# Written order on every engine, and earlier value tiles and opening steps, in a four-layer attention kernel

## The chip, the cores and the metric

The kernel runs on one core of a Trainium2 chip. The metric is the device time of one execution in microseconds (us); less is better. A program of instructions is built ahead of time: TensorE (PE) does matmuls and transposes into PSUM, VectorE (DVE), ScalarE (ACT) and GpSimd (POOL) do everything elementwise, and SyncE (SP) issues most of the DMA transfers. Each engine takes its own instructions in the order in which the program holds them and waits, at each, for what it needs from the others.

## The reference

Four layers in a row, each with a residual: linear attention (A), infini attention (B), A and B again, on x of 2048 tokens x 512 features, 32 heads of 16.

```python
def _A_ref(x, wqkv, w_phi, wo):                       # x is layer-normalized
    q, k, v = heads(x @ wqkv)                         # 32 heads, Dh = 16
    pq, pk = q @ w_phi, k @ w_phi                     # per head
    phi = lambda t: concat([softmax(t), softmax(-t)]) # 32 features a head
    kv, z = phi(pk)^T @ v, sum over tokens of phi(pk)
    return (phi(pq) @ kv / (phi(pq) @ z + 1e-6)) @ wo

def _B_ref(x, wq, wk, wv, wo, beta):                  # N = 4 segments of L = 512 tokens
    g = sigmoid(beta); M = z = 0; phi = lambda t: where(t > 0, t + 1, exp(t))
    for s in range(N):
        p = softmax(qs @ ks^T * Dh**-0.5 + causal_mask)
        a_mem = phi(qs) @ M / (phi(qs) @ z + 1e-6)
        o[s] = g * a_mem + (1 - g) * (p @ vs)
        M, z = M + phi(ks)^T @ vs, z + sum of phi(ks)
    return o @ wo

for layer in (A, B, A, B): x = x + layer(layernorm(x))
```

Inputs and outputs are fp32.

## The kernel before

Every dense product is kept near fp32 by splitting both factors into a high and a low part (fp32r) and adding three products (`mm3`): a 128 x 512 tile of a projection is 12 matmuls of 512 columns. A token tile is 128 tokens; a chunk or segment is four of them. Splitting is always an ACT copy (high) and a DVE or POOL subtraction (low). Work is written as Python generators, which other generators advance by `next`: the code that advances them decides the order in which instructions are emitted.

**Linear attention** is class `LayerA`. `pass1` goes over four chunks in the order `SEGS`. In each it projects k and q tiles (`kproj`, `qproj`), turns k tiles into features, and adds the products of features and values to `kva` (`kv(0)` after the first two k tiles, `kv(1)` after the other two). A feature tile goes through ACT's copy out of PSUM, DVE's maxima and minima (`extremes`), two POOL subtractions (`differences`), ACT's `exp`, DVE's sums, a reciprocal, and a product shared between DVE and POOL (`scale_k`). q tiles are stored to DRAM (`pqs`) with their maxima. Meanwhile a side generator normalizes the next chunk (`norm_T`: rows by DMA, moments on DVE, `refine`, `normal` on ACT, transposed into columns by PE) and makes its value tiles (`v_tile`). `first` writes out the start of the very first chunk by hand. `pass2` goes over 16 tiles of q: transposes of the features, the product with `kva`, a division (`weigh`), transposes of the result (`turn`), the output projection, and the residual.

**Infini attention** is class `LayerB`. `opening` loads the first weights of q and k (`wqk`) and all of v (`bwv`), starts the first norm and fills constant rows (`start`). `steps` walks k from `BEGIN` = -31 over R = 5 steps for each of 32 half chunks (8 heads x 512 tokens go in two halves). In each step TensorE does a fifth of the logits (`attend`, "lg") and a fifth of the products whose row maxima are taken on DVE (`maxima`, "mx"). Between them stand the tasks of a table: `BEFORE` (k < 0), `FIRST` (segment 0), `GAPS` (1 and 2), `LAST` or `FINAL` (3). A cell such as `0.4 m0` means half chunk 0, step 4, memory update 0; `v3` is a value tile, `n` and `ln` a step of the next norm, `fin` a `finish`, `max` the maxima. The tail of `steps` (after the loop) does the last `finish`, the rest of `early`, `end_turn` and `end`, together with the beginning of the next linear layer's pass1 (`after`).

`prepare` runs beside the first pass1: it splits the five weight matrices that come later into high and low parts and stores them to DRAM. `load_w` of such kept weights reads them again, `wtiles` "w8" or "e8" receiving two DMAs of 1 MB. At the end of each linear layer the main program walks pass2 for `A20` steps and advances `opening` at every third step from k = 30 on; the rest of pass2 goes into `steps` before k = 2, as far as the budget `LEFT` (in ns of TensorE work) tells.

**What sets the order.** The program is built by a framework that may reorder instructions by a timeline of its own. The class `Ordered` wraps the engines and ties each instruction behind the one before it, but only while a flag says so:

```python
j = (ends if ordered[0] or back[0] else floor).get(self.engine)
```

`strict` does the same for TensorE. The flags are on in `first`, in the last chunk of each pass1, in pass2 and in the loop of `steps`; in the first three chunks of pass1, in most of `prepare` and in the tail of `steps` the framework orders ACT, DVE, POOL and SP (and TensorE in part).

Of the kernel before, what the change touches and what calls it, by code (L numbers as in the profile page):

```python
# [15 lines left out]
D = 512  # L16
# [21 lines left out]
LEFT = 44000  # L38
BEGIN = -31
MAXIMA = -9  # L40
A20 = 76
PREP = 6
EVERY = (2, 2)
# [7 lines left out]
0.1 max k2/2       | 0.3 k2~           | 0.4 m0  # L51
1.1 max q3/2       | 1.3 fin q3~       | 1.4 t1 k3/1
# [47 lines left out]
BEFORE = {-30: "ln0", -29: "ln0", -28: "ln0", -27: "ln0", -25: "q0", -23: "v0", -21: "k0", -20: "load", -19: "v1",  # L100
          -18: "n", -17: "v2 n", -16: "n", -15: "n n", -14: "q1 n", -13: "n", -12: "v3 n", -11: "n", -10: "k1 n",
# [4 lines left out]
def interleave_kernel(ctx, tc, x_in, a_wqkv, a_wphi, a_wo, b_wq, b_wk, b_wv, b_wo, b_beta,  # L106
# [25 lines left out]
    strict = [False]  # L132
    last = [None]
    ordered = [False]
    back = [False]
    ends = {}
    floor = {}
    put_off = [None]

# [13 lines left out]
    class Ordered:  # L153


# [3 lines left out]
        def __getattr__(self, op):  # L159
            f = getattr(self.engine, op)  # L160

            def call(*a, **k):
                i = f(*a, **k)  # L163
                j = (ends if ordered[0] or back[0] else floor).get(self.engine)
                if j is not None:
                    behind(i, j)
                ends[self.engine] = i
                return i
            return call
# [3 lines left out]
    def held(i):  # L173

        if strict[0] and last[0] is not None:
            behind(i, last[0])
        last[0] = i
        return i
# [24 lines left out]
    def constants():  # L203

        sync.dma_start(out=mask, in_=c_mask)
        sync.dma_start(out=eb, in_=b_beta.unsqueeze(0).broadcast_to([P, H]))
        act.activation(eb, eb, AF.Exp, scale=-1.0)
        dve.tensor_scalar(eb, eb, 1.0, None, op0=ADD)
        dve.reciprocal(gates[:, 1, :], eb)
        dve.tensor_scalar(gates[:, 0, :], gates[:, 1, :], -1.0, 1.0, op0=MUL, op1=ADD)  # L210
        for j in range(4):
            dve.tensor_copy(share[32 * j : 32 * j + 32, :], gates[32 * j : 32 * j + 32, 0, j:H:4])
        dve.tensor_scalar(share, share, -1.0, bd[:, 24:25], op0=ADD, op1=MUL)
        dve.tensor_scalar(share, share, 1.0, None, op0=ADD)
        dve.tensor_copy(ones, bd[0:32, 25:26].broadcast_to([32, P]))
# [19 lines left out]
    def bring(w, key, src=None, tag="w8", low=dve):  # L235
        hi, lo = wtiles(tag)
        w[:] = [hi, lo]
        if key in kept:
            for t, k in zip((hi, lo), kept[key]):
                dma(t, k)  # L240
                yield
            return
# [56 lines left out]
    def prepare():  # L299


        for _ in range(PREP):
            yield
        back[0] = True
        constants()
        back[0] = False
        for m, src in enumerate((b_wq, b_wk)):
            for kc in range(NC):
                raw = T2("xr", 3)
                sync.dma_start(out=raw, in_=src[kc * P : (kc + 1) * P, :])  # L310
                hi = T2("oh", OO, F32R)
                lo = T2("ol", OO, F32R)
                for e in range(2):
                    for r in range(2):
                        rv = raw.rearrange("p (c f r e d) -> p e r c d f", c=NC, f=2, r=2, e=2)[:, e, r]
                        hv = hi.rearrange("p (c f e d r) -> p e r c d f", c=NC, e=2, f=2, r=2)[:, e, r]
                        lv = lo.rearrange("p (c f e d r) -> p e r c d f", c=NC, e=2, f=2, r=2)[:, e, r]
                        back[0] = True
                        act.copy(hv, rv)
                        back[0] = False  # L320
                        pool.tensor_tensor(out=lv, in0=rv, in1=hv.bitcast(F32), op=SUB)
                        for _ in range(EVERY[m]):
                            yield
                for a, t in enumerate((hi, lo)):
                    dma(wqk[m][:, :, a, kc, :], t.rearrange("p (c x) -> p c x", c=NC))
        for key, src in (("awo", a_wo), ("bwv", b_wv), ("bwo", b_wo)):
            keep = [dtile((P, NC, D), nm(key)) for _ in range(2)]
            for kc in range(NC):
                raw = T2("xr", 3)
                sync.dma_start(out=raw, in_=src[kc * P : (kc + 1) * P, :])  # L330
                hi = T2("oh", OO, F32R)
                lo = T2("ol", OO, F32R)
                back[0] = True
                act.copy(hi, raw)
                back[0] = False
                pool.tensor_tensor(out=lo, in0=raw, in1=hi.bitcast(F32), op=SUB)
                for k, t in zip(keep, (hi, lo)):
                    dma(k[:, kc, :], t)
                for _ in range(EVERY[1]):
                    yield  # L340
            kept[key] = keep
# [134 lines left out]
    def v_tile(hT, w, vv, tag):  # L476
# [4 lines left out]
        for t in range(4):  # L481
            po = PS(*tag)
            yield from tok_proj(po, hT, t, w)
            act.copy(v[:, t, 0 : H * VW].rearrange("p (h e) -> p h e", e=VW)[:, :, 0:DH],
                           po.rearrange("p (h e) -> p h e", e=DH))
            yield
# [80 lines left out]
    class LayerA:  # L567
# [4 lines left out]
        def first(self, hT, vv, nxt):  # L572

            ordered[0] = strict[0] = True
# [39 lines left out]
            side = norm_T(self.xsrc, SEGS[1], nxt, "e8", slow=True, off=True)  # L614
            next(side)
# [7 lines left out]
            for t in range(4):  # L623
# [5 lines left out]
                for _ in range(NEXT[t]):  # L629
                    next(side)  # L630
# [4 lines left out]
            ordered[0] = strict[0] = False  # L635
            floor.update(ends)
            return wq, wk, wv, side

        def pass1(self, first):
            hTs, vv, nxt = [], [], []  # L640
            if first:
                wq, wk, wv, ahead = self.first(hTs, vv, nxt)
# [15 lines left out]
            kva = sp.tile([P, 8, 4 * VW], F32, tag="acc", bufs=1, name=nm("kva"))  # L658
            for n, s in enumerate(SEGS):
# [3 lines left out]
                def kproj(t, e=None):  # L663
# [5 lines left out]
                    mm = extremes(pk, T2("mm", 2, shape=(P, 2, H)))  # L669
                    if e is None:  # L670
                        f = differences(pk, mm)
                        exp(f)
                        es.append(scale_k(f))
                    else:
                        e[t] = differences(pk, mm)

                def qproj(t):
# [36 lines left out]
                def go(steps):  # L714
                    for step in steps.split():
                        yield from {"k": kproj, "q": qproj, "v": kv}[step[0]](int(step[1]))

                if n < NSEG - 1:
                    hTs, vv = [], []
                    spare = ("e8" if first else "w8") if n % 2 == 0 else None  # L720
                    side = norm_T(self.xsrc, SEGS[n + 1], hTs, spare)
                    if first and n == 0:
                        hTs, side = nxt, ahead
                    side = chain(side, v_tile(hTs, wv, vv, ("g", G)))
                    steps = "k0 q0 k1 q1 v0 k2 q2 k3 q3 v1"
                    strict[0] = first and n == 0
                    if strict[0]:
                        steps = "k0 k1 q0 q1 v0 k2 k3 q2 q3 v1"
                    if n == 0 and not first:
                        yield from go("k0 k1 v0 k2 k3 v1")  # L730
                        wq = load_w("awq", None, "e8")
                        steps = "q0 q1 q2 q3"
                    if n == NSEG - 2:
                        steps, late = steps[:-3], kv(1)
                    for i, _ in enumerate(go(steps)):
                        next(side, None)
# [3 lines left out]
                    for _ in side:  # L740
                        yield
                    continue

                e = {}
                ordered[0] = strict[0] = True

                for t in range(8):
                    yield from (kproj(t, e) if t < 4 else qproj(t - 4))
# [76 lines left out]
    class LayerB:  # L825
# [6 lines left out]
        def start(self):  # L832
            self.mem = sp.tile([P, NC, 2, 8 * VW], F32, tag="acc", bufs=1, name=nm("mem"))
            self.sets = []
            for b in range(NSET):
                Q, K = [T2("e8", 2 * NSET, F32R, (P, 4, 512)) for _ in range(2)]
                self.sets.append((Q, K))
                for t, rows in ((Q, mask[0:32, 0:P]), (K, ones)):
                    dma(t[3:P:4].rearrange("p a t -> p (a t)"), rows.unsqueeze(1).broadcast_to([32, 16, P]))

# [4 lines left out]
        def values(self, s):  # L845

            self.vv[s] = []
            yield from v_tile(self.hT[s], self.wv, self.vv[s], ("g", G))
# [247 lines left out]
        def opening(self):  # L1096
# [5 lines left out]
            w = []  # L1102
            side = bring(w, "bwv")
            self.wv = w
            for _ in side:
                yield
            self.norm0 = self.norm(0)
            next(self.norm0)
            self.start()
            for _ in range(10):  # L1110
                yield
                next(self.norm0)

        def steps(self, side, after, table_end):
# [75 lines left out]
            for k in range(BEGIN, R * N + 4):  # L1190
                m = k // R + 3
                ordered[0] = k < R * N
# [27 lines left out]
                if k == R * N - 1:  # L1220
                    ordered[0] = False
                    floor.update(ends)
            put_off[0] = None
            for f in self.late + self.rows:
                f()
            next(after, None)
# [8 lines left out]
            strict[0] = False  # L1235
# [15 lines left out]
    for i in range(2):  # L1251
# [4 lines left out]
        for k in range(A20):  # L1256
            next(a2)
            if k >= 30 and k % 3 == 0:
# [35 lines left out]
```

## Time and profile before

| | |
|---|---|
| median of 3 runs | 1601.99 us (1600.36 to 1604.97) |
| the profiled execution | 1601.45 us |
| span of its profile | 1599.7 us, 28160 instructions |
| mean granted TensorE clock | 0.989 |
| TensorE busy | 95% of the span, 9856 matmul records |
| DVE, ACT, POOL busy | 71%, 49%, 40% |
| DMA | 195.70 MB, 122 GB/s on average |

The span is what the profile covers, from the first to the last instruction; 1.75 us of the execution lie outside it. The stretches of the program in this trace are: start to 36, first pass1 to 205, first pass2 to 355 (its last tiles run within the beginning of infini attention), first infini attention to 848 with the start of the second pass1 in it, second pass1 to 988, second pass2, and second infini attention to the end. In rows of instructions the name left of "<-" is what is written, the ones right of it what is read; a bracket holds the idle time of the engine before the row and what ended it. All instructions that go through a helper bear the helper's line (163 for the wrapped engines, 185 and 189 for matmuls and transposes), so tile names tell them apart: `P` is a feature tile or a probability tile, `U` and `tb` the copies of k and q, `xr`, `oh`, `ol` the tiles of `prepare`, of residuals and of `turn`, `w` weights, `hh`/`hl` and "e"/"w" buffers the normalized columns.

### The profile page before, as it was taken

How to read it: one execution, taken by the hardware profiler on the slowest of the kernel's cores; microseconds unless marked ns; L12 is line 12 of the kernel's file. 1: busy time of each engine (PE TensorE's matmuls, PEld its weight loads, DVE VectorE, ACT ScalarE, POOL GpSimd, SP SyncE). 2: the span in 40 equal slices, each digit the busy share in tenths (PEclk: the TensorE clock that was granted, in tenths of full speed). 3: DMA queues.
4: the chain of work that ended last, by engine and by line, in shares of the span. 5: the costliest groups of instructions: out<-in, count | busy, mean ns of one | idle time of the engine just before them, and what ended most of it. 6: DMA issues, size and time to landing. Idle time of an engine off the chain costs nothing.

```text
span 1599.7 us, 28160 instructions
## 1 busy us (share of the span) xinstructions
PE 1512.0 (95%) x9856; PEld 1079.1 (67%) x9856; DVE 1135.5 (71%) x3282; ACT 786.5 (49%) x1178; POOL 642.9 (40%) x976
## 2 busy tenths in 40 slices
PE   7999998988999999999999999889889999999998
PEld 6788887765666666666568888777656666666554
DVE  4675775667787887888655657647688778777784
ACT  5444333425565565555534424343455655655553
POOL 1457653413443453433222337433234444533422
PEclk9999999999999999999999999999999999999999
DMA  7348144634443543543232111743354344334331
GB/s 273 132 137 264 73 163 151 185 95 148 132 106 100 140 100 106 140 105 122 81 144 61 52 58 51 236 152 106 103 176 113 103 137 106 102 111 107 81 88 52
DMA packets 100988, 195.70 MB, mean 122 GB/s; under 512 B 13552, under 2 KB 26992, under 8 KB 97776
## 3 DMA queue, kind: packets, MB, share of 16 engines
q1 hardware_dynamic: 99696, 193.38, 40.3%
q8 instruction: 79, 1.29, 0.3%
q10 hardware_dynamic: 1152, 0.52, 0.1%
q14 instruction: 61, 0.50, 0.1%
HBM read 101.05 MB, written 39.85 MB: 88 GB/s over the span
## 4 chain that ended last, share of the span: by engine, by line
PE 67%; DVE 17%; ACT 5%; issue 5%; DMA 3%; POOL 2%; SPq 1%; DVEq 0%; ACTq 0%; POOLq 0%
PE g L185 39%; DVE mx L163 9%; PE mx L185 8%; PE lg L185 8%; PE pv L185 6%; PE g L189 6%; ACT P L163 2%; ACT tb L163 2%; DVE mxs L163 2%; POOL P L163 1%; DVE ta L163 1%; DMA x<-x 1%; DVE es L163 1%; DMA xr<-in 1%; ACT x L163 1%
## 5 line engine op out<-in xcount | busy, mean ns | idle before, releaser
L163 DVE CUSTOM_DVE_ANT_0 mx<-mx,mask 128x128 f32<-128x128 f32 (+3 forms) x1024 | 510.4, 498 | 166.0 <-PE mx L185 131.4
L163 ACT ACTIVATE P<-lg 128x1024 f32<-128x1024 f32 x320 | 328.7, 1027 | 185.6 <-PE lg L185 172.7
L163 POOL TENSOR_SCALAR_AFFINE_SELECT P<-P 128x256 f32<-128x256 f32 (+1 forms) x448 | 190.3, 439 | 439.3 <-ACT P L163 437.6
L185 PE MATMUL g<-hh,wqk 128*128 128x512 f32 x512 | 180.6, 407 | 1.8 <-ACT hh L163 1.3
L185 PE MATMUL mx<-e,e 63*128 63x256 f32 (+2 forms) x1024 | 155.6, 360 | 22.0 <-DVE mxs L163 15.8
L185 PE MATMUL lg<-e,e 64*128 64x256 f32 (+2 forms) x1024 | 168.6, 387 | 8.0 <-ACT P L163 7.1
L185 PE MATMUL g<-w,oh 128*128 128x512 f32 x512 | 172.7, 420 | 3.6 <-ACT oh L163 2.7
L185 PE MATMUL pv<-P,v 128*32 128x512 f32 (+3 forms) x2048 | 165.2, 441 | 0.0
L185 PEld LDWEIGHTS lg<-e,e 64*128 64x128 f32 x1024 | 81.2, 184 | 103.6 <-issue 53.8
L185 PE MATMUL g<-w,hh 128*128 128x512 f32 x448 | 145.9, 406 | 3.1 <-ACT tb L163 3.1
L163 DVE DVE_READ_ACCUMULATOR2_ANT mxs<- 128x1 f32 x1024 | 144.5, 141 | 0.0
L185 PEld LDWEIGHTS mx<-e,e 63*128 63x128 f32 x1024 | 82.9, 185 | 70.4 <-DVE mxs L163 49.8
L185 PEld LDWEIGHTS pv<-P,v 128*32 128x32 f32 x2048 | 53.6, 109 | 98.7 <-issue 88.1
L185 PEld LDWEIGHTS g<-hh,wqk 128*128 128x128 f32 x512 | 96.3, 188 | 23.2 <-ACT hh L163 1.8
L185 PEld LDWEIGHTS g<-w,oh 128*128 128x128 f32 x512 | 91.7, 194 | 26.8 <-ACT oh L163 4.1
L163 POOL TENSOR_SCALAR tb<-tb 128x512 f32<-128x512 f32 x48 | 71.5, 1489 | 84.7 <-ACT tb L163 84.7
L185 PE MATMUL g<-w,ol 128*128 128x512 f32 x256 | 103.3, 404 | 1.1 <-DVE ol L163 1.1
L185 PE MATMUL g<-hl,wqk 128*128 128x512 f32 x256 | 100.3, 392 | 0.4 <-DVE hl L163 0.4
L163 ACT CAST ta<-g 128x512 fp32r<-128x512 f32 x64 | 37.4, 585 | 119.4 <-PE g L185 116.4
L185 PEld LDWEIGHTS g<-w,hh 128*128 128x128 f32 x448 | 80.0, 189 | 22.2 <-ACT tb L163 5.2
L185 PE MATMUL g<-w,hl 128*128 128x512 f32 x224 | 88.5, 395 | 0.0
L163 POOL TENSOR_TENSOR P<-P,rr 128x512 f32<-128x512 f32 x32 | 34.6, 1082 | 127.3 <-DVE rr L163 127.3
(133 smaller groups left out, 2714.3 us busy)
## 6 DMA issues: line engine op xcount, KB each, us to landing
e<-ta SPq DMA_DIRECT2D x384, 128.0 KB
wqk<-wqk SPq DMA_DIRECT2D x64, 512.0 KB
x<-x SPq DMA_DIRECT2D x48, 256.0 KB
xr<-in SPq DMA_DIRECT2D x28, 256.0 KB
pq<-tb SPq DMA_DIRECT2D x24, 256.0 KB
tb<-pq SPq DMA_DIRECT2D x24, 256.0 KB
x<-xr SPq DMA_DIRECT2D x24, 256.0 KB
xr<-x SPq DMA_DIRECT2D x24, 256.0 KB
```

The source lines that it names most:

```text
L163: i = f(*a, **k)
L185: return held(nc.tensor.matmul(*a, **k))
L189: return held(nc.tensor.transpose(*a))
```

## The change

All flags go: `Ordered` ties every instruction behind the one before it on its engine, and `held` does so for TensorE, throughout the program. Then several orders are written out anew:

- pass1: one list of steps for all chunks, `kv(1)` after the first k tile of the next chunk, `exp` and `scale_k` one and two steps after their tile, value tiles woven in by threes of matmuls, the next norm's moments spread over the chunk before (`rows`), norms with `refine` on POOL. In the second layer's first chunk the weights of q are loaded during k1, and the features of the first k tiles are put aside until the infini layer before has ended (`aside`).
- prepare: the constants come first, and copy, subtraction and store of a piece are issued one step apart, with three raw pieces asked for ahead.
- `load_w` and `bring` read kept weights in eight DMAs of 256 KB.
- opening: its steps are taken at k = 6 to 21 (weights) and from k = 42 on (rows, norm, fills one by one); `A20` is 82, `LEFT` 40000.
- infini attention: the value tiles are made in the order 0, 3, 1, 2, the fourth one (tile 2) within the first half chunk; k1 and the other value tiles of `BEFORE` move, and the first memory update `m0` goes from 0.4 to 1.1.

The diff, cut to its core:

```diff
-LEFT = 44000
+LEFT = 40000
-A20 = 76
+A20 = 82
-EVERY = (2, 2)
+EVERY = 2
 FIRST = """
-0.1 max k2/2       | 0.3 k2~           | 0.4 m0
-1.1 max q3/2       | 1.3 fin q3~       | 1.4 t1 k3/1
+0.1 max k2/2       | 0.2 v3/2          | 0.3 k2~
+0.4 v3             | 1.1 max m0 q3/2   | 1.3 fin q3~       | 1.4 t1 k3/1
...
-BEFORE = {..., -20: "load", -19: "v1",
-          -18: "n", -17: "v2 n", ..., -12: "v3 n", -11: "n", -10: "k1 n",
+BEFORE = {..., -20: "load",
+          -18: "n", -17: "v1 n", ..., -12: "k1 n", -11: "n", -10: "v2 n",
 class Ordered:
-                j = (ends if ordered[0] or back[0] else floor).get(self.engine)
-                if j is not None:
-                    behind(i, j)
+                if self.engine in ends:
+                    behind(i, ends[self.engine])
 def held(i):
-        if strict[0] and last[0] is not None:
+        if last[0] is not None:
 def constants():
         sync.dma_start(out=eb, in_=b_beta.unsqueeze(0).broadcast_to([P, H]))
+        yield
 def bring(w, key, src=None, tag="w8", low=dve):
         if key in kept:
-            for t, k in zip((hi, lo), kept[key]):
-                dma(t, k)
+            for kc in range(NC):
+                for t, k in zip((hi, lo), kept[key]):
+                    dma(t[:, kc, :], k[:, kc, :])
                 yield
 def prepare():
+        yield from constants()
         for _ in range(PREP):
             yield
...
+        copied, stored = None, None
+        for piece in chain(pieces(), (None, None)):
+            if stored:
+                _, keep, tiles = stored
+                for k, t in zip(keep, tiles):
+                    dma(k, t.rearrange("p (c x) -> p c x", c=NC) if len(k.shape) == 3 else t)
+            if copied:
+                (raw, hi, lo), _, _ = copied
+                pool.tensor_tensor(out=lo, in0=raw, in1=hi.bitcast(F32), op=SUB)
+            if piece:
+                (raw, hi, _), _, _ = piece
                 act.copy(hi, raw)
+            copied, stored = piece, copied
+            for _ in range(EVERY):
+                yield
 class LayerA, pass1:
+            def upcoming(n):
+                h = []
+                spare = ("e8" if first else "w8") if n % 2 else None
+                return h, norm_T(self.xsrc, SEGS[n], h, spare, slow=True, off=True)
+            def rows(g):
+                for _ in range(11):
+                    next(g)
+                    yield
...
-                    side = norm_T(self.xsrc, SEGS[n + 1], hTs, spare)
-                    side = chain(side, v_tile(hTs, wv, vv, ("g", G)))
-                    steps = "k0 q0 k1 q1 v0 k2 q2 k3 q3 v1"
...
-                    if n == 0 and not first:
-                        yield from go("k0 k1 v0 k2 k3 v1")
-                        wq = load_w("awq", None, "e8")
-                        steps = "q0 q1 q2 q3"
+                    hTs, g = upc
+                    side = [] if n or first else [rows(g)]
+                    side += [g, v_tile(hTs, wv, vv, ("g", G))]
+                    if n + 2 < NSEG:
+                        upc = upcoming(n + 2)
+                        side.append(rows(upc[1]))
+                    side = chain(*side)
+                    def go(late):
+                        ready, done = [], []
+                        for step in "k0 k1 q0 q1 k2 v0 k3 q2 q3".split():
+                            if step == "v0":
+                                yield from kv(0)
+                                continue
+                            t = int(step[1])
+                            yield from (kproj if step[0] == "k" else qproj)(t, e)
+                            if done:
+                                es.append(scale_k(e[done.pop()]))
+                            if ready:
+                                exp(e[ready[0]])
+                                done.append(ready.pop())
+                            if step[0] == "k":
+                                ready.append(t)
+                            if step == "k0" and late:
+                                yield from late
+                    for i, _ in enumerate(go(late)):
+                        if i == 4 and n == 0 and not first:
+                            wq = load_w("awq", None, "e8")
+                        if aside[0] is None and i > 3:
+                            next(side, None)
                         if n == 1 and i % 4 == 0:
                             settle(1)
                         yield
                     for _ in side:
                         yield
+                    late = kv(1)
 class LayerB:
 def start(self):
                     dma(t[3:P:4].rearrange("p a t -> p (a t)"), rows.unsqueeze(1).broadcast_to([32, 16, P]))
+                    yield
 def values(self, s):
-            yield from v_tile(self.hT[s], self.wv, self.vv[s], ("g", G))
+            yield from v_tile(self.hT[s], self.wv, self.vv[s], ("g", G), (0, 3, 1, 2))
 def opening(self):
-            self.start()
-            for _ in range(10):
-                yield
-                next(self.norm0)
+            fills = self.start()
+            for n in (0, 0, 1, 1, 1, 1, 1, 1, 0, 1, 1, 1, 1):
+                yield
+                next(fills, None)
+                for _ in range(n):
+                    next(self.norm0)
 def steps(self, side, after, table_end):
+            aside[0] = []
             next(after, None)
             self.finish(N - 1)
...
             self.end(o)
+            for f in aside[0]:
+                f()
+            aside[0] = None
 main program:
-            if k >= 30 and k % 3 == 0:
+            if k % 3 == 0 and (5 < k < 24 or k > 41):
                 next(opening, None)
```

## The prediction

> **What bounds the kernel now.** First the head of the page, for who is busy:
>
> ```profile
> PE 1512.0 (95%) x9856; PEld 1079.1 (67%) x9856; DVE 1135.5 (71%) x3282; ACT 786.5 (49%) x1178; POOL 642.9 (40%) x976
> ```
>
> TensorE is the bound: 1599.7 - 1512.0 = 88 us of the span are its idle time. The change leaves the matmuls as they are, so it can move only these 88 us and the time lost at a low clock. Second, busy time by stretch, to see where they lie (length, busy us and count of PE, PEld, DVE, ACT, POOL; clock; DMA share; GB/s):
>
> ```profile
> 36.00:205.00 169.00, 161.79 (x836) 136.49 (x835) 111.69 (x180) 73.06 (x133) 100.52 (x103) 0.97 0.45 148
> 205.00:267.00 62.00, 56.34 (x357) 48.26 (x356) 40.93 (x89) 26.88 (x44) 28.76 (x33) 0.94 0.54 179
> 267.00:350.00 83.00, 76.90 (x439) 61.02 (x437) 52.75 (x141) 30.04 (x52) 22.74 (x28) 1.00 0.45 136
> 350.00:425.00 75.00, 66.00 (x477) 40.04 (x479) 56.60 (x194) 40.31 (x57) 28.71 (x52) 1.00 0.48 143
> 800.00:848.00 48.00, 44.19 (x249) 33.14 (x242) 25.47 (x51) 18.07 (x27) 14.96 (x20) 0.93 0.31 120
> 848.00:988.00 140.00, 138.72 (x742) 117.24 (x740) 89.04 (x151) 50.16 (x79) 53.66 (x50) 1.00 0.17 57
> 988.00:1048.00 60.00, 53.61 (x338) 46.15 (x339) 38.74 (x86) 25.33 (x41) 26.43 (x32) 0.94 0.56 184
> 1048.00:1150.00 102.00, 91.91 (x529) 70.62 (x527) 64.82 (x179) 37.90 (x62) 27.76 (x36) 1.00 0.44 131
> 1150.00:1225.00 75.00, 69.50 (x522) 42.19 (x523) 58.75 (x205) 44.01 (x62) 31.43 (x58) 1.00 0.45 133
> ```
>
> Length minus PE is the idle time. By program: first pass1 7.2, second 1.3; the starts of pass2 5.7 and 6.4; then the passage into infini attention 6.1 + 9.0 and 10.1 + 5.5. Third, the same view on single gaps' surroundings, for the clock:
>
> ```profile
> 232.13:243.72 11.59, 9.47 (x64) 7.83 (x62) 5.57 (x13) 5.23 (x8) 5.76 (x6) 1.00 1.02 403
> 243.72:250.54 6.82, 5.96 (x18) 5.09 (x19) 6.55 (x16) 0.00 (x0) 1.53 (x2) 0.50 1.02 263
> 250.54:265.75 15.21, 12.89 (x83) 10.91 (x83) 9.07 (x19) 8.36 (x14) 7.03 (x13) 1.00 0.38 124
> 90.11:96.94 6.83, 6.83 (x27) 5.94 (x26) 5.64 (x11) 1.94 (x4) 2.33 (x6) 0.50 0.13 38
> ```
>
> After some gaps the clock is halved, here for 6.8 us twice, and each such stretch loses up to half its length. The timeline shows the two gaps before them and a third, at 827:
>
> ```profile
> 244.58 1.98 PE L185 MATMUL g<-KN,P 128*128 128x68 f32 x8 [2.05 <-DVE xr L163]
> 243.00 0.69 DVE L163 BATCH_NORM_STATS2 bs<-x 128x6 f32<-128x512 f32 x1 [3.46 <-DMA x<-x]
> 79.90 4.49 DVE L163 TENSOR_TENSOR P<-P,es 128x512 f32<-128x512 f32 x1
> 87.94 0.74 PE L185 MATMUL mx<-v,P 128*128 128x68 f32 x5 [2.08 <-DVE P L163]
> 827.38 1.08 PE L189 MATMUL g<-ident,tmp 128*128 128x128 f32 x4 [2.86 <-ACT P L163]
> ```
>
> **Starts of pass2: -14.** An undisturbed iteration of pass2 takes 6.04 us (208.60 to 214.64). Eight of them should take 48.3 us; from 208.60 to the first column step at 265.75 they take 57.15, a loss of 8.8. The rows above make it up: idle 2.1 + 0.9 + 2.3, and half of 6.8 at the halved clock. Cause: opening() puts two wqk loads (512 KB), bwv (2 x 1 MB), four rows and four fills (256 KB each) on SP's queue between 228 and 243, while DMA moves 403 GB/s; moments 0 is called three steps after its rows and holds DVE 3.46 us, with all that is queued behind it. Pass2 of the second layer loses 57.85 - 48.3 = 9.5. After, the 3 MB of weights go out at k=6..21, about 12 us, which is 250 GB/s beside the base of some 125 GB/s in undisturbed pass2; rows leave at k=42, moments come 9 steps later, and one fill goes out per call. refine to normal 0 gets six steps instead of three. I leave a loss of 1.7 in each (late residuals during the weights, 1.0; moments, 0.7): (8.8 - 1.7) + (9.5 - 1.7) = 14.9, rounded down to 14. Ends -17 (nothing left) and -6 (the burst costs half as much as it did).
>
> **First pass1: +1.5.** Before loses 7.2 idle and half of 10.2 us at half clock (3.4 at 42.3, 6.8 at 90.1): 12.3. After, three things stall.
> (a) The ten small DVE operations of constants() (3.25 us) now stand ahead of the maxima of k0 and delay column 2 of the next norm by about 2.2; the gap that stood there was 2.16 (39.49 to 41.65) and halved the clock for 3.4. Kept: 2.2 + 1.7.
> (b) kv(1) of a chunk comes after k0 of the next one. Its last feature tile runs, in the present second layer:
>
> ```profile
> 911.15 0.59 ACT L163 COPY tb<-g 128x512 f32<-128x512 f32 x1 [2.42 <-PE g L185]
> 911.77 1.28 DVE L163 TENSOR_REDUCE mmq<-tb 128x32 f32<-128x512 f32 x2 [1.73 <-ACT tb L163]
> 912.97 1.21 DVE L163 TENSOR_REDUCE es<-P 128x64 f32<-128x1024 f32 x1
> 914.21 0.55 DVE L163 RECIPROCAL es<-es 128x64 f32<-128x64 f32 x1
> 914.91 1.08 POOL L163 TENSOR_TENSOR P<-P,es 128x512 f32<-128x512 f32 x1 [3.30 <-DVE es L163]
> ```
>
> Scaling of k3 is written behind q3's maxima, so from the end of q3's matmuls to scaled features is 911.15 to 915.99, some 5 us, and TensorE has k0 to do, 12 x 0.2325 = 2.8. That is 2.3 to 2.5 of stall at each boundary where no value tile lies between: twice here (first to second and second to third chunk), 5.0, and 2.0 each for the clock (between none and 3.4): 4.0.
> (c) prepare() now copies one step, subtracts the next, stores the one after; a copy that needs a buffer waits on ACT for a store issued two pieces before, and ACT's PSUM copies queue behind it. At 1.5 steps of slack against transfers of 2.6 to 4 us in the crowded part, 1.0 (0 to 6).
> Sum 2.2 + 1.7 + 5.0 + 4.0 + 1.0 = 13.9, so +1.6; ends -5 (no halved clock, no (c)) and +8.
>
> **Second pass1: +3.5.** It idles only 1.3 now. One bare boundary is added, 2.4 + 2.0, and 0.4 for refine on POOL; less 1.3. Ends 0 and +7.
>
> **End of the first infini layer: -4.** At 827 end_turn waits 2.86 (the row names P; what ended last is the sum of finish(31) on DVE, at 826.81 behind 1.2 of maxima and a 1.21 reduction of the next layer's key tiles), then 0.67, then the clock is halved until 834.2. After, these features are put aside until end(o) is out, finish comes 3 matmuls after weighted instead of 12, and early's nine and k1's six matmuls lie before end_turn: 1.1 of 3.5 left, -2.4; gaps of 0.9 to 1.5 at 357 to 398 left the clock at 1.00, so half of the 3.4 goes: -1.7. Ends -6 and 0.
>
> **Start of infini attention: -4.** In 350 to 425 and 1150 to 1225 TensorE waits for DVE's maxima and ACT's exponentials, 9.0 and 5.5. The fourth value tile (2.8 of matmuls) moves there out of a stretch before k=0 that is fuller; about half covers a wait: -1.5 in each layer; -0.5 each for k1, v1, v2 and normal 0 coming earlier. Ends -6 and +1. The memory update m0 two gaps on costs nothing: m1 follows a half chunk later, and no reader of it comes before the next chunk; with that cover gone, its 0.4 us copy.
>
> **Loads in 256 KB pieces: 0.** 54 more issues of 0.33 to 0.6 us on SP, 6 per load, put a load's last piece 2 to 3 us later; the wq load has some 8 us until its use. Ends 0 and +2.
>
> **Sum.** 1.5 + 3.5 - 14 - 4 - 4 = -17. The profiled execution took 1601.45 (1.75 outside the span), 0.5 under the median: about 1585.
>
> **Rivals.** *The clock stays up.* The 2.05 and 2.08 us gaps were followed by a halved clock, one of 2.00 at 259 was not (its row shows 1.00), so a stall of 2.4 may leave it up as well. Without the three 2.0 and 1.7 of (a): about 1577. The Trainium skill's "TensorE: Matmul & The Clock Gate", HAM oscillation, has the clock fall only after idle gaps above some 3.4 us; by that rule 1577 would be the forecast, but the trace's 2.05 us speaks against it.
>
> *The burst only moves.* At k=6..21 the weights may delay residuals and query tiles that have 6 us from issue to use; loads took 5 to 8 us in the old burst. Then the openings gain 2 and not 14, all else as above: about 1597 to 1601. Against it: 3 MB in 12 us, where the old burst had 5 MB in 15.
>
> *Written order stalls pass1 (slower).* Nothing may overtake a waiting instruction: POOL's differences and refine stand behind subtractions that wait for ACT's copies, which wait for stores. The 4.49 us DVE product above ran while POOL was busy without pause until 83.85; beside less it took 0.68 at 828.85. If this falls on the kv chain, each boundary costs 5 + 3.4 instead of 4.4 (+12 over three), and (c) reaches its 6 us with a halved clock (+8); with the openings at their poor end (+8) this gives 1613. It decides once pass1 loses 17 us more than the sum has. Against it: DVE was busy 66% and POOL 59% of the first pass1, POOL 38% of the second. The Trainium skill's "SBUF — State Buffer", Who interferes with whom, says that DVE with two SBUF inputs and GpSimd lock each other out for a whole instruction; the 4.49 us row agrees, and it speaks against moving refine to POOL.
>
> *No such order.* If the compiled order were as before outside the openings, only -14 remains: 1588; little speaks for it.
>
> **Numbers.** The sum 0.45 (its own range 1578 to 1594), clock up 0.18, burst moved 0.15, slower 0.17, no such order 0.05. A measurement tells 0.3%, 4.8 us, from no change. Burst moved splits 0.03 faster, 0.10 same, 0.02 slower; of the last case 0.02 counts as faster, 0.01 same, 0.02 slower. Faster 0.68, same 0.11, slower 0.21. The range leaves out most of the slow rival and 0.05 at the low end: 1574 to 1606.
>
> **What would show it.** Right: pass2's eight iterations take 50 us, not 57; DVE never waits 3 us for x there; PE waits some 2.4 us for P at each kv(1) after a k0, then shows 0.50; the gap at 827 is near 1. Wrong: waits of 2 us or more for xr or tb early in pass2, ACT waiting for stores of ol and oh in pass1, or pass1 above 180 us.

## The result, and the profile after

The changed kernel takes 1656.02 us (median of 6 runs, 1651.18 to 1662.12); the kernel before, in as many runs beside it, 1604.32. The ratio is 1.0329, interval 1.0300 to 1.0359: 52 us slower by the medians, where 17 us faster was forecast. The profiled execution took 1657.15, its span 1655.0, 55.3 more than before.

The head of the page, then busy time by stretch. The stretches are cut at the same instructions in both kernels: first pass1 from its first k tile to pass2; the first pass2 until the columns of the infini norm; the last 16 us of the first infini layer up to end_turn; from there the second pass1.

```profile
PE 1537.8 (93%) x9856; PEld 1098.8 (66%) x9856; DVE 1130.6 (68%) x3252; ACT 787.5 (48%) x1178; POOL 652.6 (39%) x1006
```

```profile
36.58:236.32 199.74, 172.35 (x836) 143.92 (x835) 105.53 (x169) 73.17 (x133) 103.26 (x118) 0.90 0.44 147
83.87:104.35 20.48, 11.65 (x49) 10.96 (x50) 6.94 (x10) 6.87 (x15) 8.86 (x17) 0.50 0.72 268
145.31:158.96 13.65, 10.39 (x46) 10.00 (x47) 5.50 (x8) 1.82 (x4) 8.64 (x10) 0.50 0.54 151
236.32:296.85 60.53, 56.31 (x376) 47.91 (x375) 43.36 (x95) 29.08 (x46) 30.09 (x34) 1.00 0.60 191
298.91:305.73 6.82, 6.14 (x17) 4.63 (x18) 1.92 (x3) 1.17 (x2) 0.72 (x3) 0.50 0.00 0
835.73:851.35 15.62, 15.62 (x97) 11.20 (x95) 4.99 (x10) 3.60 (x6) 2.11 (x4) 1.00 0.45 155
851.35:1042.43 191.08, 171.35 (x829) 144.51 (x827) 107.79 (x170) 58.81 (x91) 69.54 (x80) 0.90 0.14 49
```

The same two pass1 of the kernel before, and between them its last stretch up to end_turn:

```profile
36.27:205.39 169.12, 161.91 (x835) 136.48 (x834) 111.88 (x181) 73.00 (x133) 100.54 (x104) 0.97 0.45 148
807.78:827.38 19.60, 16.74 (x101) 11.61 (x98) 10.99 (x25) 6.24 (x10) 6.64 (x10) 1.00 0.29 108
827.38:986.83 159.45, 157.63 (x825) 133.10 (x826) 101.52 (x174) 56.65 (x88) 59.23 (x56) 0.98 0.17 57
```

The first pass1 takes 199.74 instead of 169.12, the second 191.08 instead of 159.45: +30.6 and +31.6, more than the whole loss. In the first, idle time goes from 7.2 to 27.4, and TensorE's busy time grows by 10.4 for the same matmuls, since the clock is at 0.90; in the second from 1.8 to 19.7, and by 13.7. Elsewhere the change gains: the 15.6 us before end_turn took 19.6 and have no gap any more (2.9 of the 4.0 us are idle time, the rest is less matmul time in the stretch).

Where a stall comes from is seen at the first boundary of chunks. TensorE's timeline at kv(1), then ACT's in the stretch before (rows left out at ...):

```profile
83.87 0.69 PE L180 MATMUL mx<-v,P 128*128 128x68 f32 x2 [2.40 <-POOL P L159]
93.39 2.83 PE L180 MATMUL mx<-v,P 128*128 128x68 f32 x12 [8.83 <-POOL P L159]
```

```profile
77.92 0.46 ACT L159 ACTIVATE st<-st 128x4 f32<-128x4 f32 x2 [2.90 <-DVE st L159]
...
78.50 0.63 ACT L159 COPY tb<-g 128x512 f32<-128x512 f32 x1
79.03 1.05 ACT L159 ACTIVATE P<-P 128x1024 f32<-128x1024 f32 x1
85.47 0.81 ACT L159 ACTIVATE x<-x,st 128x512 f32<-128x512 f32 x1 [5.38 <-POOL st L159]
...
88.04 0.61 ACT L159 COPY tb<-g 128x512 f32<-128x512 f32 x1
```

Read upwards: q3 is copied out of PSUM (second `tb<-g`) at 88.04, 9.4 us after its last matmul ended at 78.67. Ahead of it in ACT's written order stand normals of the next norm (`x<-x,st`), the first of which waited 5.38 for refine. On POOL refine (`st`) stands behind scale_k's product:

```profile
82.30 1.51 POOL L159 TENSOR_TENSOR P<-P,es 128x512 f32<-128x512 f32 x1 [4.44 <-DVE es L159]
83.78 0.49 POOL L159 TENSOR_TENSOR st<-st 128x4 f32<-128x4 f32 x2
```

That product waited for DVE's sums, those stood behind q2's maxima, and q2's copy (78.50) had waited on ACT behind root (77.92) for DVE's moments. So one chain runs through three queues, and only after q3's copy do q3's maxima, the features of k3 and kv(1) come. kv(1) gets to its first product with k3's features at 93.39, 11.9 us after k0 ended, and the clock is at 0.50 until 104.35.

### The profile page after: what moved, and what is told of

It reads as the page before. It is cut to its first block, busy times and chain, and to the rows that moved or that the text cites. A ratio compares the mean times of both kernels' runs of the same rounds, so it can differ in the third digit from the quotient of the medians.

```text
span 1655.0 us, 28160 instructions
## 1 busy us (share of the span) xinstructions
PE 1537.8 (93%) x9856; PEld 1098.8 (66%) x9856; DVE 1130.6 (68%) x3252; ACT 787.5 (48%) x1178; POOL 652.6 (39%) x1006
## 4 chain that ended last, share of the span: by engine, by line
PE 64%; DVE 19%; issue 5%; ACT 5%; POOL 3%; DMA 3%; SPq 1%; ACTq 0%; POOLq 0%; DVEq 0%
PE g L180 36%; PE mx L180 8%; DVE mx L159 8%; PE lg L180 7%; PE g L184 6%; PE pv L180 6%; POOL P L159 2%; DVE es L159 2%; ACT P L159 2%; DVE mxs L159 1%; ACT tb L159 1%; DVE bs L159 1%; DVE mmq L159 1%; DVE ta L159 1%; DMA x<-x 1%
## 5 line engine op out<-in xcount | busy, mean ns | idle before, releaser
L180 PE MATMUL g<-w,hh 128*128 128x512 f32 x448 | 149.5, 415 | 5.8 <-DVE ta L159 5.0
L159 DVE TENSOR_REDUCE mmq<-tb 128x32 f32<-128x512 f32 x64 | 40.9, 681 | 72.6 <-ACT tb L159 72.6
L159 POOL TENSOR_TENSOR P<-P,es 128x512 f32<-128x512 f32 x32 | 49.1, 1534 | 103.3 <-DVE es L159 103.0
```

The source lines that it names most:

```text
L180: return held(nc.tensor.matmul(*a, **k))
```

## The experiments

Single runs here scatter by some 5 us (the changed kernel's six by 11). The medians of the kernel before beside them are 1600 to 1606.

**Is it the order, or the new places of the steps?** Two runs cross the two: the old places with all flags on, and the new places with the old flags back.

```
e4 (before):  strict = [True]; ordered = [True], never reset
e5 (after):   j = (ends if ordered[0] else floor).get(self.engine)   # flags as in before
```

(In e5 prepare's copies on ACT, which the kernel before ties too, stay free.)

> The kernel before with its flags always on: every engine in written order, the old places of all steps. Theory W (written order itself costs, with any list of steps that was not made for it): kv(1) stands right behind q3 and waits for the whole 5 us chain of its features, and normals and copies wait in ACT's order; 15 to 35 us slower than before, 1615 to 1640, all of it in the two pass1. Theory N (the new places of the steps cost, not the order): within 5 us of before, 1597 to 1607.

> The changed kernel with the old flags: in the first three chunks of both pass1, in prepare and in the tail of the infini layers the framework may reorder again; the new places of the steps stay. Theory W: ACT may copy q out of PSUM before the normals, and TensorE may do columns and projections before kv(1); pass1 returns to 165 to 175 us and 140 to 150, time 1590 to 1605. Theory N: pass1 stays above 190 and 165, time above 1640.

The old places go from 1600.4 to 1782.9 when written in order, the new ones from 1591.9 to 1656.0. Theory W holds on both sides: written order costs 182 us with the old list and 64 with the new one, which is much better made for it. That is why the change as a whole loses. The size of e4 was expected far too low, 15 to 35.

**Is it where the next norm stands?** Three edits of the changed kernel move the norm that stood ahead of q3's copy.

```
e1:  rows(): for _ in range(11) -> range(5)      # root, refine, normals in the next chunk
e2:  norm_T(..., slow=True, off=True) -> off=False   # refine on DVE
e10: rows(): range(11) -> range(1)               # all of the norm in the next chunk
```

> The changed kernel, but rows() takes 5 steps of the next norm instead of 11: the moments stay in the chunk before, and root, refine and the four normals come at the head of the next chunk's side work. Theory O (order on ACT): pass1 lost time because root and normal stand in ACT's queue ahead of q2's and q3's copies out of PSUM and wait there for DVE and POOL; here the tail of a chunk holds none of them, so the stalls of 11.2 (at 81 to 93) and 7.4 us (141 to 149) at kv(1) fall to the 2.4 that the prediction had, and the gap of 5.5 at 179 goes: first pass1 from 199.7 to 175 to 183 us, second from 176 to 155 to 165, time 1610 to 1632. Rival K (kv(1) has too little work ahead of it, whatever ACT does): stalls as now, time 1650 or more.

> The changed kernel, with refine of pass1's norms on DVE instead of POOL, all else in its place. Theory P (POOL is to blame: refine waits there behind POOL's half of scale_k): the normals no longer wait, time 1610 to 1630. Theory O (the place in the order is to blame): on DVE refine stands behind the other half of scale_k, which ends 0.9 us earlier than POOL's; the normals come at most 1.5 us earlier at each of some six places, time 1642 to 1656.

> The changed kernel, all in written order, but rows() takes 1 step of the next norm instead of 11: only its DMAs go out a chunk ahead; moments, root, refine and normals all come in the chunk whose columns they make, between k0 and the value tiles. Theory O+D (waits in written queues: on ACT root and normals, on DVE moments that stand ahead of q3's maxima): nothing of the norm stands ahead of k3's features any more, so the stall at kv(1) falls to its own 2.4 to 3; the gap of 5.5 at 179, which is ACT waiting for prepare's stores, stays. First pass1 from 199.7 to 178 to 186, second from 176 to 152 to 162, time 1612 to 1630. If the norm's place does not matter: 1645 or more.

1662.1, 1659.9 and 1659.6: none gains anything. e2 is as theory O said, e1 and e10 miss its times. In e1 the first stall falls from 11.2 to 4.2, but at the next boundary the moments, now behind scale_k of k2, hold q3's maxima on DVE, for stalls of 2.8 and 5.7, and behind a copy of prepare kv(0) waits 8.4. In e10 the stall at kv(1) has fallen to 3.2 at the first boundary and 2.5 at the second, as computed from its own chain, but others, of 3.0 and 6.3, have come at the columns. The stall at the first kv(1), and the longest at the columns:

```profile
84.46 1.79 PE L180 MATMUL mx<-v,P 128*128 128x68 f32 x13 [3.18 <-POOL P L159]
162.08 1.12 PE L184 MATMUL g<-ident,x 128*128 128x128 f32 x4 [6.26 <-ACT tb L159]
```

There the copies out of PSUM stand behind normals once more, and behind copies of prepare. Moving one step moves the wait.

**Which queue?** Freed or tied one by one, in the stretches that were free before:

```
e6:  TensorE free, the rest written      e7:  ACT free
e14: ACT and DVE free                    e8:  TensorE written, the rest free
e15: ACT written, the rest free
```

> The changed kernel, but in the stretches that were free before (three chunks of each pass1, prepare, tails) the framework may reorder TensorE, and TensorE alone; ACT, DVE, POOL and SP stay in written order. Theory T (what costs is that kv(1) stands fixed in TensorE's queue with nothing allowed past it): columns and projections go ahead of kv(1), most of the 64 us between the changed kernel and its free version come back, 1595 to 1615. Theory O (the waits pile up in ACT's queue, where copies out of PSUM stand behind prepare's copies, root and normals that wait for DMA, DVE and POOL): three PSUM buffers are full all the same, at most 10 us come back, 1645 to 1658.

> The changed kernel, but in those stretches ACT alone may be reordered; TensorE, DVE, POOL and SP stay in written order. Theory O: most of the 64 us come back, what is left is kv(1)'s own chain, 2.4 us a boundary and the halved clock after it: 1600 to 1620. Theory T: no more than 10 us, 1645 to 1658. A third theory, that the orders of several engines hold each other (DVE's moments wait for rows, POOL's refine for scale_k): 1620 to 1645 here and in the run with TensorE free.

> The free version of the changed kernel (1591.9 us in one run), with TensorE alone kept in written order there. Theory T: it loses most of the 64 us, 1635 to 1656. Theory O: it stays near, up to three bare kv(1) stalls of 2.4 us with 2 for the clock, 1590 to 1606.

> The changed kernel with ACT and DVE free in the stretches that were free before; TensorE, POOL and SP in written order. With ACT alone free it took 1622.7, with all but TensorE free 1610.1. If DVE's order (moments ahead of the maxima) is the second wait: 1608 to 1615, near the latter. If POOL's or SP's order holds it: 1618 to 1625, near the former.

> The free version (1591.9) with ACT alone kept in written order there. Theory O: ACT's order is enough by itself to lose half or more of the 64 us, 1622 to 1650, with stalls of 4 us and more at kv(1) and at columns. Third theory (only several orders together cost): the others move around ACT's waits, 1592 to 1610.

| free there | us | both pass1 in the trace |
|---|---|---|
| nothing (changed kernel) | 1656.0 | 390.8 |
| TensorE (e6) | 1649.8 | 376.6 |
| ACT (e7) | 1622.7 | 363.0 |
| ACT, DVE (e14) | 1605.9 | 341.8 |
| ACT, DVE, POOL, SP (e8) | 1610.1 | 340.2 |
| all but ACT (e15) | 1605.2 | 334.5 |
| all (e5) | 1591.9 | 322.4 |

Freeing ACT alone returns 33 of the 64 us, DVE with it 17 more, and TensorE the last 14 to 18; POOL and SP add nothing beyond scatter. Tying ACT alone costs only 13. The two pass1 by themselves, 328.6 in the kernel before, give the same order: ACT 28 of 68 us, DVE 21, TensorE 18 to 19. So theory T falls, theory O names the largest part, and the third theory is nearest: the price comes from several written queues that hold each other. With all free the same copy of q3 comes at 83.28, some 2.5 us after its matmuls, and TensorE does columns while kv(1) waits:

```profile
83.28 0.58 ACT L162 COPY tb<-g 128x512 f32<-128x512 f32 x1
83.40 0.33 PE L184 MATMUL mx<-v,P 128*128 128x68 f32 x2
83.57 1.04 PE L188 MATMUL g<-ident,x 128*128 128x128 f32 x8
```

**What does prepare add?** Near 180 in the changed kernel TensorE waits 5.54 for a copy that stands on ACT behind prepare's:

```profile
184.26 1.22 PE L180 MATMUL g<-w,e 128*128 128x512 f32 x2 [5.54 <-ACT tb L159]
183.11 0.62 ACT L159 CAST oh<-xr 128x512 fp32r<-128x512 f32 x1 [8.19 <-DMA bwv<-oh]
183.63 0.58 ACT L159 COPY tb<-g 128x512 f32<-128x512 f32 x1
```

```
e11 (on e10): three steps for each of the last twelve pieces instead of two
e18 (after):  prepare's copies, subtractions and DMAs not tied behind anything
```

> The same, with three steps instead of two for each of prepare's last twelve pieces (786 KB each). If ACT's gap at 179 is prepare's copy waiting for the store of a piece before (its buffers are a ring of three), slower pieces find their buffer free: 4 to 9 us less than the run without it, all in the first pass1. If that gap comes from somewhere else: within 2 us.

> The changed kernel, all in written order but prepare's copies, subtractions and their DMAs, which the framework may put anywhere. If prepare's copies, waiting in ACT's order for stores to land, cost what the first pass1's third and fourth chunk take more than the second layer's (59.4 and 64.6 us against 49.8 and 54.3 between first k tiles): those fall by 12 to 20 in all, the second pass1 stays, time 1636 to 1645. If the second layer's causes explain the first too: 1650 to 1658.

e11 took 1649.4, 10 less than e10, but its first pass1 is 2.2 longer, not shorter; the difference lies in later stages, so it shows nothing of prepare. e18 took 1645.5: the third chunk falls from 64.6 to 57.3 and the gap near 180 is gone, while the second chunk (60.4; the expectation counts these two as fourth and third) and the second pass1 stay. Prepare's wait for its stores is worth 7 us of the third chunk, and the first pass1 as a whole falls by 5.6, to 194.1, of the 31 that it had lost: less than expected.

**What are the opening and the tables worth by themselves?** Each alone on the kernel before:

```
e16: opening(), start() one fill per call, calls at k = 6..21 and from 42,
     A20 = 82, LEFT = 40000, kept weights in 8 pieces
e17: FIRST, BEFORE and the order 0, 3, 1, 2 of the value tiles
```

> The kernel before with only the new opening: its calls at k = 6 to 21 and from 42, A20 82, LEFT 40000, kept weights in eight pieces, one fill per call. By the prediction's sum: 14 us less, 1586 to 1590. By the trace of the changed kernel, where pass2 gained 3.4 and 5.2 us because the columns then waited behind DVE and halved the clock: 6 to 10 us less, 1592 to 1597. If the opening only shifts its waits: 1599 to 1605.

> The kernel before with only the new tables: the value tiles in the order 0, 3, 1, 2, the fourth of them in the first half chunk, k1 and the others of BEFORE moved, m0 at 1.1. By the prediction: the start of infini attention gains 4 us in the two layers, 1596 to 1600. By the traces so far (the last turn of pass2 to attend 4 takes 56.2 us, or 59.1 with a halved clock, with the new tables, and 54.3 to 56.5 with the old ones): 0 to 8 us slower, 1602 to 1610.

The opening alone gives 1591.07 against 1604.14, ratio 0.9894 (0.9857 to 0.9932), 11 to 23 us faster. The tables alone give 1608.56 against 1602.88, ratio 1.0037 (1.0015 to 1.0060), 2 to 10 us slower. In e17's trace the waits that the tile was to cover are shorter, as meant (from the third to the ninth exponential of the first half chunk TensorE idles 1.7 us instead of 3.0), but where the value tile was taken away, before k = 0, pass2's next transposes wait 2.1 and 1.2 instead of 1.5 and 0.5, and now the clock falls:

```profile
291.24 0.73 PE L189 MATMUL g<-ident,P 128*128 128x128 f32 x4 [2.14 <-ACT tb L163]
293.12 1.11 PE L189 MATMUL g<-ident,tmp 128*128 128x128 f32 x4 [1.15 <-ACT v L163]
```

```profile
291.70:301.94 10.24, 9.02 (x32) 6.78 (x31) 4.42 (x11) 4.48 (x8) 4.92 (x5) 0.50 0.19 53
```

**Variants of the free version.**

```
e9 (on e5):  the old FIRST, BEFORE and order of the value tiles
e12 (on e5): A20 = 85
e13 (on e5): both
```

> The free version with the old tables BEFORE and FIRST and the old order of the value tiles, so that the fourth value tile is made before k = 0 again and m0 stands at 0.4; A20 and LEFT stay. From the last turn of pass2 to attend 4 the free version takes 59.1 us in each layer and the kernel before 54.8. If the tables cost what this stretch lost: back to about 55 in both and 8 us less in all, 1583 to 1586. If the tables are neutral and the 4 us came with LEFT and A20, which put other work into that stretch: no change, 1590 to 1594. The prediction had the tables gain 4 us: then 1594 to 1597.

> The free version with A20 = 85: pass2 is walked to the end of an output projection instead of its first three matmuls, before the columns of the first infini norm. In the changed kernel column 0 waits 1.4 and column 2 and the next projection 0.8 and 0.7 behind DVE there, and the clock is halved for 6.8 us after them, in both layers. If the place of the columns is what gave the gain at the start of pass2 back: those gaps and the halved clock go, 3 to 6 us a layer, 1580 to 1587. If those waits come from the burst of fills and rows whatever A20 is: no change, 1589 to 1595.

> The free version with A20 = 85 and the old tables: the opening, the end of the infini layers and the new pass1 steps stay, the written order and the new tables go. Sum from single runs: 1591.9, less 3 to 6 a layer for A20, less 0 to 3 a layer for the tables: 1576 to 1587, faster than both kernels. If what A20 gives is taken back at the start of the infini layer: 1589 to 1594.

1591.7 and 1595.0 in single runs. e9's stretch from pass2's last turn to attend 4 fell from 59.1 to 56.3 and 56.5, but the run's first pass1 was 4 us longer, so its total decides nothing; e12 is a miss: the gaps at the columns are gone, and gaps of 2.5 and 1.2 at pass2's tile 10 with 10.2 us at half clock have taken their place. e13, in six runs, takes 1585.84 against 1602.83, ratio 0.9896 (0.9869 to 0.9924): faster than both kernels. So is the opening alone, and the two intervals do not tell these apart.

## Why the prediction was wrong, by its steps

| term | forecast | trace after minus before |
|---|---|---|
| first pass1 | +1.5 | +30.6 |
| second pass1 | +3.5 | +31.6 |
| starts of pass2, two layers | -14 | -3.4 and -5.2 |
| start of infini attention, two layers | -4 | +1.4 and +4.3 |
| end of the first infini layer | -4 | -4.0 |

In the traces pass2 is taken here from its start to its last turn, the start of infini attention from there to attend 4. Two of the signs that the prediction named for being wrong came: pass1 above 180 us, and ACT waiting for stores of `oh` in it.

**First and second pass1, step (b), failed, and with it the sign.** It took the chain from q3's last matmul to scaled features, 5 us, from a trace in which the framework had chosen the order, and let the copy of q3 start at once. In written order that copy came 9.4 us after the matmuls. The steps of the next norm, whose emission the prediction listed only as refine on POOL for 0.4, stand ahead of it on ACT. Instead of 2.4 a boundary, TensorE stalled 11.2 and 7.4 at kv(1) in the first layer and 6.7 in the second, where kv(0) waited 2.6 and the columns 5.9 and 3.8 for normals, for which the sum had nothing beyond the 0.4; each time with a halved clock beside it. The chain by itself was sized well: in e10, where none of the norm's steps stands ahead of k3's features, kv(1) stalls 3.2, 2.5 and 2.5. But there the same steps hold the columns, and the two pass1 gain less than 4 us together.

**Step (c)** was right in kind and too small: 1.0 forecast, 6 as its bound; 5.5 of gap in the trace with 6.8 us at half clock beside it, and 5.6 of the first pass1 by e18. **Step (a)** was too high: 1.1 instead of 2.2, and no halved clock.

**The slow rival** had the sign and the kind, and it named refine behind other POOL work and copies behind stores; but it gave 1613, since it added a fixed sum to each boundary and did not follow who waits on whom through three queues. The slow DVE product beside a busy POOL (4.49 us) that it leaned on did not come up: scale_k's products took 0.69 on DVE and 1.51 on POOL at the stall.

**Starts of pass2: right in kind, too high.** The burst went as forecast: DVE no longer waits 3.5 us for x there, nor TensorE behind it. But the stretch to the columns still idles 4.2 us, and after it the columns wait 1.4 and 0.8 with 6.8 us at half clock; the prediction had left 1.7. e16, the opening alone, is 11 to 23 us faster for a forecast of 14, but that does not bear the step out: of the 9.7 us that its trace gains only 2.4 and 4.0 lie between the start of pass2 and attend 4 of the two layers, and its columns too are followed by a halved clock. Where the rest comes from stays open.

```profile
266.92:273.74 6.82, 5.95 (x17) 4.44 (x18) 2.14 (x4) 1.21 (x3) 0.94 (x3) 0.50 0.00 0
```

**Start of infini attention failed in sign.** The value tile covers waits where it has gone to, 1.2 of its 2.8 us in e17, near the half that was computed, but it had covered others where it stood; "a stretch that is fuller" was read from the trace with the tile still in it. For m0 no wait shows: between 385 and 425 TensorE waits only for maxima, exponentials and reciprocals of divisions. It was not run alone.

**End of the infini layer: right in kind.** The waits of 2.86 and 0.67 and the half clock behind them are gone. That the table shows the forecast -4.0 is partly luck: the stretch ends at end_turn, so it holds 2.9 us of the wait and 1.1 of matmul time that moved; what was gained behind it, the 0.67 and the clock, is in the second pass1. With written order the second layer's first norm then stalls 5.9 us; freed (e5) it does not.

**The clock rival** fell: in e10, where the stalls at kv(1) are bare, 3.2, 2.5 and 2.5 us, each was followed by a halved clock.

## What to carry to other kernels

A list of steps that was emitted for a reordering framework is not an order to run: before tying a queue, walk each engine's list and ask of every instruction that waits (on ACT a normalization, on DVE a statistic, on POOL a correction) which copies out of PSUM stand behind it. A chain read from a reordered trace says nothing of what written order puts ahead of it, and here moving a single step moved the wait to the next queue. Freeing the queues gave the time back; spreading all the steps anew within a written order was not tried. When filler work is moved into a gap, price the place it leaves as carefully as the place it enters.

## What the runs showed of the hardware

The clock fell after short gaps that lay close together. In e5 two gaps of 0.7 us (342.71 to 343.41 and 344.14 to 344.83) within one stretch, in which TensorE was busy 2.02 of 3.41 us, were followed by 3.41 us at half clock, though the same two gaps at the same place of the changed kernel's first layer were not:

```profile
341.63:345.04 3.41, 2.02 (x13) 1.13 (x10) 3.00 (x10) 1.50 (x2) 0.41 (x1) 1.00 0.57 161
345.04:348.45 3.41, 3.41 (x9) 2.62 (x9) 0.00 (x0) 0.00 (x0) 0.00 (x0) 0.50 0.00 0
```

So the length of one gap does not decide it. The Trainium skill's "TensorE: Matmul & The Clock Gate", HAM oscillation, gives idle gaps above some 3.4 us as the condition; these rows do not agree. In every trace here the half clock begins and ends on one grid of 3.41 us. The same pair of gaps was followed by it only where both lay within one step of the grid, as here and in the changed kernel's second layer (step 1182.96 to 1186.37); in that kernel's first layer a step ends at 380.83, within the second gap. But in e16's first layer both lie in one step (345.43 to 348.84), with TensorE busy for the same 2.02 us, and the clock stayed up. So neither the gap nor the busy share of a step decides alone, and what does was not settled here.
